# Larger backward loads, a padded copy of wo, and backward stores issued by GpSimd, in a transformer block's forward and backward kernel

**Chip, cores, metric.** One core of one Trainium2 chip. Times are device microseconds (us) of that core for one execution; a median is quoted with the lowest and the highest run. TensorE is the matmul engine (PE in the profile, PEld its weight loads), VectorE is DVE, ScalarE is ACT, GpSimd is POOL, SyncE is SP (SPq: its queue of DMA issues). The granted clock is the share of TensorE's full clock that the chip allowed.

## The reference

A block of layer norm, 16-head attention (head size 28) and a gated MLP, side by side, on 2048 rows of 448 values. The kernel returns the output and the gradients of the input and of all five weight tensors, in bf16.

```python
S, D, H, F = 2048, 448, 16, 1792
xn = layernorm(x)
y  = x + attention(xn, wqkv) @ wo + (silu(xn @ w_gate) * (xn @ w_up)) @ w_down
out, vjp = jax.vjp(f, x, wqkv, wo, w_gate, w_up, w_down)
grads = vjp(grad_out)
```

## The kernel before

A forward pass spills what the backward pass needs to device memory. Then come 512 backward steps, 128 for each of four groups of heads: ScalarE forms two exponentials, VectorE multiplies them by the backward scores into a tile `ds_sb`, and a DMA transposition, or TensorE for every fourth step, makes `dsT` of it. Between the steps other work is filled in: first the output y, then weight gradients and the gradient of the input. SyncE issues all DMAs that matter here, the transpositions among them. Loads are registered with a due step and dripped into its queue; stores are held for two steps.

```python
def drop():                      # once per step
    ...
    while slow and credit > 0:
        _, _, o, i = slow.pop(0)
        SP.dma_start(out=o, in_=i)
        credit -= size(o)

def load_q(g, qc):
    t = new_q(g, qc)
    drip(("q", g, qc), [(t[:, i:i + 2], QD_d[g, qc, :, i:i + 2]) for i in (0, 2)], 128 * g + 4 * qc - 4)

def store(o, i):
    held.append((now + 2, o, i))
    flush(0 if now < NB else 10 ** 9)

def flush(upto):
    while held and held[0][0] <= upto:
        _, o, i = held.pop(0)
        SP.dma_start(out=o, in_=i)

def dst_dma(b, ds, qi):          # three steps of four
    if qi == 0:
        dsT[b] = bk.tile([P, 4, 2, 4, P], BF16, name="dsT", bufs=3)
    SP.dma_start_transpose(out=dsT[b][:, qi].rearrange("p j kt s -> p (j kt) s"),
                           in_=ds[:].rearrange("p j k -> p (j k)"))

# in ew(k), the elementwise part of a step
ds = dss[k - 1] = kq.tile([P, 2, 512], BF16, name="ds_sb", bufs=10)
for j in range(2):
    DVE.tensor_tensor(out=ds[:, j], in0=dps.pop((k - 1, j))[:], in1=est[k - 1][:, j], op=ALU.mult)

# in y_unit, 16 times
y = yp.tile([P, D], BF16, name="y")          # a pool of two buffers
DVE.tensor_tensor(out=y[:], in0=ps[:, :D], in1=yts[ti][:], op=ALU.add)
store(out0_d[:, 4 * ch + ti, :], y[:])
```

The softmax here doesn't subtract the row's maximum and nothing guards it: scores larger than these inputs give would overflow.

## Time and profile before

| | before |
|---|---|
| time, median of three runs | 1447.26 us (1446.37 to 1447.65) |
| profiled span, granted TensorE clock | 1448.2 us, 0.985 |
| busy share PE, DVE, ACT, POOL | 92%, 80%, 87%, 25% |

VectorE's 80% is an average that hides its 92.5% in the later backward steps: each stretch must be read by itself.

### The profile page before, as it was taken

Reading aid. Unit: us, or ns where it says so; the run is one execution under the profiler, and the core shown is the slowest. Engines: PE = TensorE matmul, PEld = TensorE weight load, DVE = VectorE, ACT = ScalarE, POOL = GpSimd, SP = SyncE. Lnnn points to the kernel's source line nnn. Section 1 sums busy time; section 2 is a strip of 40 time slices with the busy share of each in tenths; the row PEclk is TensorE's granted clock in tenths of the full one; section 3 lists DMA queues with packets and bytes.
Section 4 is the critical chain, followed back from the end, with each engine's and each line's share of the span. In section 5 each row is a group of like instructions: output and inputs, shape, how many; then the busy total and the mean of one; then the engine's idle time right before and its main releaser. Section 6 shows DMA issues by size and latency. Waiting matters only on the chain. (4 is left out here: it accounts for less than half of the span.)

```text
span 1448.2 us, 34787 instructions
## 1 busy us (share of the span) xinstructions
PE 1335.4 (92%) x12708; PEld 539.9 (37%) x12708; DVE 1151.7 (80%) x1997; ACT 1261.2 (87%) x2193; POOL 363.1 (25%) x486
## 2 busy tenths in 40 slices
PE   5899999999999999889899989999999999999996
PEld 2333333333333333333333433433343344443343
DVE  6677756666667666488898988888889999989988
ACT  5788988988999999778898988899989999989974
POOL 6475514453344453110101101101001011010005
PEclk9999999999999999989999999999999999999998
DMA  6797947796778676799999999999999999999971
GB/s 153 161 211 184 220 112 166 177 203 154 157 170 184 143 175 145 193 211 204 217 218 211 208 225 181 211 211 212 232 193 192 208 215 230 199 197 201 204 145 60
DMA packets 701763, 271.18 MB, mean 187 GB/s; under 512 B 620224, under 2 KB 676248, under 8 KB 701592
## 3 DMA queue, kind: packets, MB, share of 16 engines
q1 hardware_dynamic: 696616, 262.83, 88.5%
q0 software_dynamic: 3568, 5.83, 1.8%
q8 instruction: 100, 1.64, 0.5%
q14 instruction: 71, 0.58, 0.1%
q10 hardware_dynamic: 1408, 0.30, 0.1%
HBM read 65.04 MB, written 59.90 MB: 86 GB/s over the span
## 5 line engine op out<-in xcount | busy, mean ns | idle before, releaser
L840 DVE TENSOR_TENSOR ds_sb<-db,e_sb 128x512 bf16<-128x512 f32 x1024 | 646.8, 684 | 54.7 <-issue 25.5
L834 ACT ACTIVATE e_sb<-sb 128x512 bf16<-128x512 f32 x1024 | 555.0, 612 | 66.1 <-PE db L818 49.8
L611 ACT ACTIVATE eT<-s_w 128x1024 bf16<-128x1024 f32 x256 | 263.5, 1029 | 47.0 <-PE s_ps L608 44.0
L613 ACT ACTIVATE eT<-s_ps 128x512 bf16<-128x512 f32 x512 | 280.5, 613 | 0.0
L818 PE MATMUL db<-kd,qd 32*128 32x512 bf16 x1024 | 236.1, 385 | 7.2 <-DVE ds_sb L840 6.4
L810 PE MATMUL sb<-kd,qd 32*128 32x512 bf16 x1024 | 210.7, 388 | 7.4 <-DMA qd<-QD_d 3.5
L959 POOL TENSOR_TENSOR dq_acc<-dq_acc,dq_st 128x256 f32<-128x256 f32 x64 | 46.4, 726 | 571.6 <-ACT dq_st L957 571.6
L917 PE MATMUL acc<-ds_sb,qd 128*32 128x512 bf16 x1024 | 161.1, 391 | 0.0
L913 PE MATMUL acc<-e_sb,qd 128*32 128x512 bf16 x1024 | 159.0, 391 | 1.3 <-DVE dw_o L527 1.3
L900 ACT COPY dsT<-db 128x1024 bf16<-128x1024 bf16 x128 | 130.2, 1017 | 14.1 <-PE db L895 13.5
L379 POOL TENSOR_TENSOR nn<-nn,ag 128x512 f32<-128x512 f32 x56 | 71.2, 1271 | 249.6 <-DVE ag L377 240.9
L608 PE MATMUL s_ps<-QQ,KK 32*128 32x512 bf16 x512 | 125.3, 385 | 3.9
L1127 PE MATMUL genb<-wguT,dau_c 128*128 128x448 bf16 x448 | 117.5, 355 | 6.3 <-ACT dq_st L957 3.9
L608 PE MATMUL s_w<-QQ,KK 32*128 32x512 bf16 x512 | 100.3, 387 | 11.8 <-ACT eT L611 10.2
L810 PEld LDWEIGHTS <-qd 32*128 32x128 bf16 x1024 | 48.2, 91 | 152.4 <-issue 140.6
L420 PE MATMUL gen<-xn_t,f_sp 128*128 128x448 bf16 x416 | 91.8, 354 | 2.6 <-DVE nn L394 1.7
L944 PE MATMUL genb<-dsT,kd 128*32 128x256 bf16 x2048 | 79.1, 274 | 6.0 <-DVE y L1079 4.2
L420 PEld LDWEIGHTS <-f_sp 128*128 128x128 bf16 x640 | 55.7, 98 | 75.9 <-issue 32.0
L895 PE MATMUL db<-ident_bf,ds_sb 128*128 128x128 bf16 x1032 | 79.0, 220 | 1.1 <-DVE ds_sb L840 1.1
L895 PEld LDWEIGHTS <-ds_sb 128*128 128x128 bf16 x1032 | 67.9, 98 | 24.6 <-issue 6.0
L380 POOL TENSOR_TENSOR nn<-nn,tt 128x512 f32<-128x512 f32 x56 | 72.0, 1286 | 4.4
L450 PE MATMUL gen<-eT,VS 128*32 128x512 bf16 x1024 | 68.4, 384 | 4.3 <-DVE nn L394 2.2
(163 smaller groups left out, 1879.5 us busy)
## 6 DMA issues: line engine op xcount, KB each, us to landing
F_d<-hda SPq DMA_DIRECT2D x56, 384.0 KB
dau_c<-F_d SPq DMA_DIRECT2D x56, 256.0 KB
h_c<-F_d SPq DMA_DIRECT2D x24, 256.0 KB
qd<-QD_d SPq DMA_DIRECT2D x24, 256.0 KB
dsT<-ds_sb SPq DMA_TRANSPOSE x383
dc<-dqkvT_d SPq DMA_DIRECT2D x12, 384.0 KB
wT_d<-wT_f SPq DMA_DIRECT2D x14, 256.0 KB
KD_d<-qk_sp SPq DMA_DIRECT2D x7, 512.0 KB
```

The source lines that it names most:

```text
L420: PE.matmul(ps[:, :D], lhsT=fsp[fc][:, t // 4, w, t % 4, :], rhs=rhs[:, t, :], start=(t == 0), stop=(t == NT - 1))
L608: PE.matmul(sp4[hh], lhsT=KK[g][r:r + HP, kt * P:(kt + 1) * P], rhs=QQ[g][r:r + HP, qsl], start=True, stop=True, tile_position=(r, 0))
L611: ACTE.activation(out=e2[0][:], in_=wide[:], func=ACT.Exp, scale=SCALE)
L613: ACTE.activation(out=e2[1][:, j], in_=sp4[2 + j], func=ACT.Exp, scale=SCALE)
L810: PE.matmul(s_ps[:], lhsT=qside[g, qc][r:r + HP, 0, qi * P:(qi + 1) * P], rhs=kside[g, kc][r:r + HP, 0, :], start=True, stop=True, tile_po ...
L818: PE.matmul(d_ps[:], lhsT=qside[g, qc][r:r + HP, 1, qi * P:(qi + 1) * P], rhs=kside[g, kc][r:r + HP, 1, :], start=True, stop=True, tile_po ...
L834: ACTE.activation(out=est[k][:, j], in_=sps.pop((k, j))[:], func=ACT.Exp, scale=SCALE)
L840: DVE.tensor_tensor(out=ds[:, j], in0=dps.pop((k - 1, j))[:], in1=est[k - 1][:, j], op=ALU.mult)
L895: PE.transpose(ps[:, c, :], ds[:, c // 4, (c % 4) * P:(c % 4 + 1) * P], ident_bf[:])
L900: ACTE.copy(out=o, in_=ps[:])
L913: PE.matmul(a[r:r + HP, :], lhsT=sp4[:, 1, r:r + HP], rhs=e[:, j, :], start=first, stop=last, tile_position=(0, r), skip_group_check=True)
L917: PE.matmul(a[r:r + HP, :], lhsT=sp4[:, 0, r:r + HP], rhs=ds[:, j, :], start=first, stop=last, tile_position=(0, r), skip_group_check=True)
```

## The change

Its intent is to take issues off SyncE: loads in one to three pieces in place of two to five, and all stores that go through `flush` issued by GpSimd. `wo`, which was loaded in four pieces into a zeroed tile, is written once in padded form to device memory in the forward pass and loaded in one piece.

```diff
+    wo_d = dram.tile([P, G, D], BF16)
...
             woT_load(3)
+            SP.dma_start(out=wo_d[:], in_=wo_pad[:, :, :D])
...
-        drip(("q", g, qc), [(t[:, i:i + 2], QD_d[g, qc, :, i:i + 2]) for i in (0, 2)], 128 * g + 4 * qc - 4)
+        drip(("q", g, qc), [(t[:], QD_d[g, qc])], 128 * g + 4 * qc - 4)
...
-        drip(("k", g, kc), [(t[:, 0:2], KD_d[g, kc, :, 0:2]), (t[:, 2], KD_d[g, kc, :, 2])], 128 * g + 16 * kc - 4)
+        drip(("k", g, kc), [(t[:], KD_d[g, kc])], 128 * g + 16 * kc - 4)
...
             _, o, i = held.pop(0)
-            SP.dma_start(out=o, in_=i)
+            POOL.dma_start(out=o, in_=i)
...
-                               for a, b in ((0, 2), (2, 4), (4, 6), (6, 7))], due)
+                               for a, b in ((0, 4), (4, 7))], due)
...   (x, o, fT, w_down, the gate and up weights and dau likewise in bigger pieces)
-    POOL.memset(wo_sb[:], 0.0)
-    drip(("y", 0, 1), [(wo_sb[HP * pv(hh):HP * pv(hh) + DH, :, :], wo_v[hh]) for hh in range(4)], 50)
+    drip(("y", 0, 1), [(wo_sb[:], wo_d[:])], 50)
```

More of the change, by code (lines that the diff above doesn't have):

```diff
@@ L871 @@
     w2 = bk.tile([P, 4, 2, P], BF16, name="dqT", bufs=1)
-    drip(("f",), [(fT[:, sc], fT_d[:, sc]) for sc in range(4)], 10)
+    drip(("f",), [(fT[:, a:a + 2], fT_d[:, a:a + 2]) for a in (0, 2)], 10)
     def late_dw(c):
@@ L1038, in load_y @@
             x_c = yp.tile([P, 4, D], BF16, name="x_c")
-            drip(("y", ch, half), [(x_c[:, a:a + 2], x_d[:, 4 * ch + a:4 * ch + a + 2, :]) for a in (0, 2)], due)
+            drip(("y", ch, half), [(x_c[:], x_d[:, 4 * ch:4 * ch + 4, :])], due)
             ych[ch, 2] = x_c
@@ L1042, in load_y @@
             o_c = yp.tile([P, G, 512], BF16, name="o_c")
-            drip(("y", ch, half), [(o_c[:, a:a + 2], OT_d[ch, :, a:a + 2]) for a in (0, 2)], due)
+            drip(("y", ch, half), [(o_c[:], OT_d[ch])], due)
             ych[ch, 3] = o_c
@@ L1047 @@
     wo_sb = yp.tile([P, G, D], BF16, name="wo_sb", bufs=1)
-    POOL.memset(wo_sb[:], 0.0)
     wd_v = B_w_down.rearrange("(fc p) d -> p fc d", p=P)
-    drip(("y", 0, 0), [(wd_sb[:, a:a + 2, :], wd_v[:, a:a + 2, :]) for a in (0, 2, 4, 6)], 35)
+    drip(("y", 0, 0), [(wd_sb[:, a:a + 4, :], wd_v[:, a:a + 4, :]) for a in (0, 4)], 35)
     load_y(0, 0)
     load_k(0, 2)
-    drip(("y", 0, 1), [(wd_sb[:, a:a + 2, :], wd_v[:, a:a + 2, :]) for a in (8, 10, 12)], 50)
-    drip(("y", 0, 1), [(wo_sb[HP * pv(hh):HP * pv(hh) + DH, :, :], wo_v[hh]) for hh in range(4)], 50)
+    drip(("y", 0, 1), [(wd_sb[:, a:a + 3, :], wd_v[:, a:a + 3, :]) for a in (8, 11)], 50)
+    drip(("y", 0, 1), [(wo_sb[:], wo_d[:])], 50)
     load_y(0, 1)
@@ L1104, in load_w @@
         w = dxs["w", fq] = dxs["pool"].tile([P, 5, 2, D], BF16, name="wguT")
-        drip(("dx", 0, fq), [(w[:, i - f0], wT_d[:, i, :, :D]) for i in range(f0, f1)], due)
+        drip(("dx", 0, fq), [(w[:, i - f0:min(i + 2, f1) - f0], wT_d[:, i:min(i + 2, f1), :, :D]) for i in range(f0, f1, 2)], due)
     def load_dx(ch, fq):
@@ L1111, in load_dx @@
         d = dxs["pool"].tile([P, 5, 2, 512], BF16, name="dau_c")
-        drip(("dx", ch, fq), [(d[:, i - f0], F_d[ch, :, i, 1:3, :]) for i in range(f0, f1)], now + 16)
+        drip(("dx", ch, fq), [(d[:, i - f0:min(i + 2, f1) - f0], F_d[ch, :, i:min(i + 2, f1), 1:3, :]) for i in range(f0, f1, 2)], now + 16)
         dxs[ch, fq] = d
```

## The prediction

> **What bounds the kernel now.** I read the page first (shares, forty slices), then cut the span into stretches, then the waits, then the queue of the engine that the change relieves. The backward pass is 512 steps, each with two exponentials on ScalarE and two multiplications by the backward scores on VectorE (tile ds_sb), and it fills about 620 to 1400 us. The first fence has, per stretch, the busy time of PE, PEld, DVE, ACT and POOL, the granted clock and the DMA share.
>
> ```profile
> 650.00:900.00 250.00, 229.56 (x2586) 94.02 (x2583) 220.07 (x358) 220.11 (x408) 21.77 (x30) 0.97 1.08 209
> 1000.00:1300.00 300.00, 288.34 (x3341) 122.55 (x3341) 277.53 (x472) 275.64 (x516) 26.85 (x37) 1.00 1.09 208
> ```
>
> Three engines are near full in both: no single one is the bound. But the early stretch, where the forward output y is computed between the steps, is looser: TensorE is 91.8% busy against 96.1%, VectorE 88.0% against 92.5%, ScalarE 88.0% against 91.9%. Counting ds_sb multiplications, the early stretch has 322 in 250 us, so 1.55 us a step; 1000 to 1300 us has 398 in 300 us, 1.51 us a step; 1100 to 1200 us has 139 in 100 us, 1.44. GpSimd is nearly idle (21.8 of 250 us). So something costs the early stretch some per cent, and a granted clock of 0.97 is only part of it.
>
> The waits of that stretch that a DMA ended (us in total, times, longest) are few:
>
> ```profile
> DVE y L1079 <- DMA out_dram<-y: 5.7, 3, 2.3
> DVE ds_sb L840 <- DMA dsT<-ds_sb: 5.0, 6, 1.7
> PEld L810 <- DMA kd<-KD_d: 2.5, 1, 2.5
> PEld L1071 <- DMA o_c<-OT_d: 1.3, 1, 1.3
> PEld L944 <- DMA dsT<-ds_sb: 1.2, 2, 0.9
> ```
>
> From 900 to 1400 us the same list names a single wait on a DMA, of 0.4 us. Why are they late here? SyncE's queue, in order of time (start, us, what):
>
> ```profile
> 837.86 1.23 SPq L827 DMA_TRANSPOSE dsT<-ds_sb  x1
> 839.14 0.58 SPq L767 DMA_DIRECT2D kd<-KD_d  x1
> 839.81 1.23 SPq L827 DMA_TRANSPOSE dsT<-ds_sb  x1
> 841.10 0.58 SPq L767 DMA_DIRECT2D kd<-KD_d  x1
> 841.78 1.45 SPq L827 DMA_TRANSPOSE dsT<-ds_sb  x1
> 843.28 0.57 SPq L767 DMA_DIRECT2D h_c<-F_d  x1
> 843.95 1.23 SPq L827 DMA_TRANSPOSE dsT<-ds_sb  x1
> 845.23 0.58 SPq L800 DMA_DIRECT2D out_dram<-y  x1
> 845.90 1.24 SPq L827 DMA_TRANSPOSE dsT<-ds_sb  x1
> ```
>
> One issue follows the other with some 0.05 us between: the queue is never empty. A transposition takes SyncE 1.23 us at least, a plain copy 0.57. Summed over 650 to 900 us: 121 transpositions 168 us, 108 copies 64 us, semaphore instructions 3 us, and about 0.05 us around each of them; that is the whole 250 us. The tile y shows the lag (duration in ns least, median and greatest, then first and last start in us):
>
> ```profile
> L1079 DVE TENSOR_TENSOR y<-genb,yt x16: 625/625/626, 707.6 to 895.9; 128x448 bf16<-128x448 f32 x16
> L800 SPq DMA_DIRECT2D out_dram<-y x16: 570/574/668, 719.2 to 902.4; - x16
> ```
>
> The first y is finished at 708.2 us and its store is issued at 719.2: 11 us, of which the program's own two-step delay is 3. I also matched every transposition with the multiplication that makes its input. In the five 50 us slices from 650 us on, the issue starts on average 9.2, 7.0, 6.5, 8.3 and 6.1 us after the input is ready; from 1100 to 1200 us it is 0.6 and 1.5. With 2.2 us (median) from the end of the issue to the landing, one in ten lands over 14.5 us after its input in the slice from 650. The ring of ds_sb has ten buffers, so one comes round after ten steps of 1.55 us, 15.5 us. The backlog therefore just reaches the ring, and that is the 5.0 us line. The waits that are put down to "DVE ds_sb" on SyncE's own list (81.6 us in this stretch) I don't believe: that input had been ready for 6 to 9 us.
>
> **What the Trainium skill says.** "DMA: Bandwidth & Descriptors", section "Issuing engines are not separate DMA queues": all DMAs run on the same 16 engines whoever issues them, and another issuer saves only sequencer time, which is usually small beside the DMA. The trace agrees that the sequencer's time is all there is to save (an issue of 0.57 us against 1.7 us more to the landing of a y store), but here that time is not small: the sequencer is full. The same page, "SWDGE vs HWDGE vs iDMA": GpSimd's descriptors are written by software on its cores, so those stores occupy GpSimd. In the trace GpSimd spends 0.53 to 0.84 us on each of its forward loads, which land 3.1 to 4.2 us after issue. "SBUF — State Buffer", section "SBUF: two separate sides": such a DMA can starve while VectorE holds the shared port pair in a two-port mode. The 1024 multiplications read one operand from PSUM, and nothing in the trace before shows such a stall; I count it as a risk.
>
> **The change, part by part.** I compared the two instruction orders. TensorE, VectorE and ScalarE run the same instructions in the same order; only their waits differ.
>
> - Stores to GpSimd: 24 dkv, 12 dqT, 16 y, 16 dwq_o and 8 last weight gradients, 76 issues. Off SyncE: 76 x 0.57 = 43 us. Onto GpSimd: 76 x 0.53 to 0.84 = 40 to 64 us, spread over 800 us in which GpSimd is 9% busy. Its additions into dq_acc (726 ns each, one per four steps) may now stand behind a store for a microsecond; ScalarE needs the buffer dq_st again only some 6 us later, so this is hidden.
> - Bigger loads: dau 56 to 32, h 32 to 16, k 28 to 14, q 24 to 12, weights 14 to 8 and 7 to 4, x and o 8 to 4 each, fT 4 to 2, and wo 4 to 1: 185 to 97. 88 x 0.57 = 50 us off SyncE. Bytes stay the same and SyncE's issue time hardly depends on size (0.37 to 0.57 us for up to 0.9 MB). Each load is placed within a few steps of where it was, some earlier (the k block before step 112 goes at 91).
> - Padded wo: one memset of 1.6 us on an idle GpSimd goes, one 448 KB store joins the forward pass, where no engine waits for it: 0.
>
> Between the first y load and the opening of the next phase (steps 17 to 180) SyncE's copies fall from 110 to 36, so 74 x 0.62 us, with the gap, = 46 us less work in some 250 us. Its demand falls to about 82%, and the backlog should go from 6 to 9 us to 1 or 2, as at 1100 us. Then the five waits above vanish: 5.7 + 5.0 on VectorE and 2.5 + 1.3 + 1.2 on TensorE, 15.7 us. Some fall while another engine has work queued, and part comes back as a wait on the next engine, so I take 70%: 11 us. As a cross-check: 161 steps at 1.51 instead of 1.55 us save 7 us; at 1.44 they save 18. Later than 900 us SyncE has a backlog of 0.5 to 4 us that holds up nobody: 0 to 2 us, I take 1. The end (1400 us on) is VectorE's chain; its four dwq_o stores move into gaps of 1.05 to 1.55 us between GpSimd's pairs of final additions: 0. Sum: 1447 - 12 = 1435 us.
>
> **Rivals.** (1) The backlog never mattered, transfers are hidden anyway, and the early stretch is slow for its clock (0.97) and its y work. For it: the recorded waits are only 15.7 us, 1% of the time, and each may sit beside other slack. Against it: the stretch lacks 4% on all three engines at once. It would give 1444 to 1448. (2) The step was SyncE's all along, and the whole early stretch falls to 1.44 us a step, with some gain to 1050 us too: 18 + 5 us, so 1424. Against it: VectorE would have to be 95% busy, as it is only in the best slice (47.64 of 50 us from 1150), and the clock is lower here. (3) GpSimd becomes the new queue: a store waits in order for its producer or for an earlier landing, dq_acc comes late, ScalarE stalls on dq_st, or larger loads in one piece hold transpositions back at the DMA engines, which are over 100% busy by the page's account (overlapping packets). It would give 1450 to 1465. Against it: 91% idle time, 6 us of slack, unchanged bytes.
>
> **Range and chances.** From the middle of 1435 down to the second rival, 1424, and up to the first with a little of the third, 1447. A gain of over 2% needs 1418 or less, 29 us, which is more than the early stretch can lose even at the best pace seen: 4%. A loss of over 2% needs rival 3 in full and more: 2%. Within 2%: 94%.
>
> **What would show it.** Right: SyncE shows real gaps from 650 to 900 us; y stores are issued 3 to 5 us after their y and by GpSimd; no wait on dsT, y or kd in that stretch; about 335 multiplications there in place of 322, and nearly the same count as before from 1100 us on. Wrong: SyncE idle and the step count unchanged (rival 1); ScalarE waiting for GpSimd's dq_acc, or landings of transpositions well over 2.2 us after issue (rival 3); a gain spread evenly over all stretches, which would mean that the queue delayed things in a way that my list of waits doesn't show.

## More of the kernel before

The page's list of DMA queues has, per queue, packets, megabytes, and the share of the 16 DMA engines' time. The hardware queue carries what SyncE issues, the software queue what GpSimd issues.

```profile
q1 hardware_dynamic: 696616, 262.83, 88.5%
q0 software_dynamic: 3568, 5.83, 1.8%
```

So SyncE's queue carries nearly all the traffic.

## The result and the profile after

The changed kernel is correct and took 1441.29 us (median of 4 runs, 1439.69 to 1441.88), against 1447.45 us (1446.37 to 1451.47, 4 runs) for the kernel before in the same rounds: a ratio of 0.9951, 95% interval 0.9930 to 0.9971. Ratios here are the mean time of one kernel's runs over that of the other's of the same rounds, so not quite the ratio of the medians. The forecast was 1435.0 with a range from 1424 to 1447: the gain was 6 to 7 us in place of 12. Both profiled runs are fast ones with the same mean clock, 0.985 (spans 1448.2 and 1440.1 us).

The two stretches of the prediction, in the kernel after (busy us of PE, PEld, DVE, ACT, POOL, then clock, DMA share, GB/s):

```profile
650.00:900.00 250.00, 234.83 (x2684) 97.87 (x2680) 227.32 (x374) 227.37 (x421) 41.48 (x66) 0.99 1.15 217
1000.00:1300.00 300.00, 288.42 (x3332) 122.26 (x3328) 278.27 (x474) 274.88 (x513) 40.69 (x60) 0.99 1.08 206
```

The early stretch rose from 229.6 to 234.8 us on TensorE and from 220.1 to 227.3 on VectorE; the later one stands where it was. Counted as in the prediction, by 50 us slices, the early stretch has 332 `ds_sb` multiplications where it had 322. The waits that a DMA ended, from 620 to 900 us (us in total, times, longest), are down to this:

```profile
DVE ds_sb L842 <- DMA dsT<-ds_sb: 3.4, 4, 1.0
PE genb L946 <- DMA dsT<-ds_sb: 0.2, 1, 0.2
```

The waits on y, kd and o_c are gone, 9.5 us by the prediction's list. The tile y (duration ns least, median, greatest; first and last start us):

```profile
L1080 DVE TENSOR_TENSOR y<-genb,yt x16: 624/624/626, 702.7 to 886.3; 128x448 bf16<-128x448 f32 x16
L802 POOL DMA_DIRECT2D out_dram<-y x16: 557/557/579, 705.2 to 889.3; - x16
DMA to landing us min/median/max: 2.8/4.4/6.0
```

The first y is done at 703.3 us and GpSimd issues its store 1.9 us later, where SyncE took 11 us. But SyncE's own queue did not become loose (start us, us, what; neighbouring issues of one kind are joined):

```profile
702.01 0.58 SPq L769 DMA_DIRECT2D h_c<-F_d  x1
702.69 6.83 SPq L829 DMA_TRANSPOSE dsT<-ds_sb  x4
709.57 0.58 SPq L769 DMA_DIRECT2D h_c<-F_d  x1
710.25 4.71 SPq L829 DMA_TRANSPOSE dsT<-ds_sb  x3
715.01 0.58 SPq L769 DMA_DIRECT2D x_c<-in_A_x_dram  x1
715.70 5.36 SPq L829 DMA_TRANSPOSE dsT<-ds_sb  x3
```

There are still no gaps, although only one copy comes to about three transpositions. Four transpositions take 6.83 us, 1.7 us each, three take 5.36. The tile view of the transpositions from about 650 to 900 us says the same (least, median and greatest ns), first before, then after:

```profile
L827 SPq DMA_TRANSPOSE dsT<-ds_sb x121: 1231/1240/2838, 650.3 to 899.7; - x121
```

```profile
L829 SPq DMA_TRANSPOSE dsT<-ds_sb x126: 1231/1377/3667, 647.8 to 899.1; - x126
```

The least is the same, the median is longer by 0.14 us and the greatest by 0.8. The page's queues after:

```profile
q1 hardware_dynamic: 672576, 255.35, 87.1%
q0 software_dynamic: 7024, 13.82, 4.1%
```

**Where the time came from.** I laid the 512 steps of the two traces side by side, by the end of each step's second multiplication, and followed the lead of the kernel after. Up to step 32 it is 0.6 us and constant. It then grows where the kernel before stood waiting: by 6.5 us between steps 32 and 64 (the ring of `ds_sb`, then y), 1.9 at 96 to 104 (y), 2.1 at 136 to 144 (kd) and 1.5 at 168 to 176 (y), 12.0 in all, and to 9.6 at step 176. In between the steps mostly take the same time in both. But it also shrinks: by 1.6 us between steps 64 and 96, 0.8 between 104 and 136, 0.5 between 144 and 168, 2.9 in all. These losses come at 742 to 749, 798 and 844 to 857 us of the trace after. Three of VectorE's four remaining waits on `dsT` lie just before them (0.8 us at 741, 0.9 at 797, 0.6 at 836); the fourth (1.0 at 773) has no loss beside it. Another 1.6 us are lost by step 300, where the clock after dips to 0.93 (900 to 925 and 1000 to 1025 us). From there to the end the lead stands at 8.0 us: 0.6 + 12.0 - 2.9 - 1.6, rounded.

A rival for part of the 12.0 us is the clock. From 650 to 900 us it stood at one half for 13.6 us before (6.8 from 673 us, 3.4 from 779, 3.4 from 844) and for 3.4 us after, means of 0.97 and 0.99. The later dips after, of 3.4 us each, go with losses of some 1 us each. By that measure up to 3 of the 12.0 us may be the clock's, an estimate; no run separates them. That the change gains at all rests on the ratios over many runs, not on this pair of traces.

### The profile page after: what moved, and what is told of

It reads as the page before. It is cut to its first block, busy times and chain, and to the rows that moved or that the text cites. A ratio compares the mean times of both kernels' runs of the same rounds, so it can differ in the third digit from the quotient of the medians.

```text
span 1440.1 us, 34682 instructions
## 1 busy us (share of the span) xinstructions
PE 1326.3 (92%) x12647; PEld 541.0 (38%) x12708; DVE 1151.8 (80%) x1997; ACT 1261.5 (88%) x2193; POOL 403.6 (28%) x561
## 3 DMA queue, kind: packets, MB, share of 16 engines
q1 hardware_dynamic: 672576, 255.35, 87.1%
q0 software_dynamic: 7024, 13.82, 4.1%
```

## The experiments

Twelve kernels ran, in three batches, each on one chip with runs of the kernel before. All gave correct results, the added stores going to a scratch tensor. The chips differ by a few us, so only ratios within a batch are compared.

| kernel | ratio to before | 95% interval | median us (before in the same batch) |
|---|---|---|---|
| stores to GpSimd alone | 0.9965 | 0.9942 to 0.9987 | 1445.21 (1451.47) |
| bigger loads and padded wo alone | 0.9992 | 0.9976 to 1.0009 | 1449.33 (1451.47) |
| before, four y buffers | 1.0005 | 0.9983 to 1.0027 | 1450.85 (1451.47) |
| after, 74 tiny stores on SyncE, early | 1.0005 | 0.9988 to 1.0023 | 1452.47 (1451.47) |
| after, 74 tiny stores on SyncE, late | 1.0014 | 0.9990 to 1.0038 | 1454.43 (1450.31) |
| after, 11 ds_sb buffers | 0.9929 | 0.9907 to 0.9951 | 1442.60 (1450.31) |
| after, loads on GpSimd too | 1.0283 | 1.0250 to 1.0316 | 1496.48 (1450.31) |
| stores alone, small loads on GpSimd too | 1.0360 | 1.0315 to 1.0405 | 1509.76 (1450.31) |
| after, 74 tiny stores on GpSimd, early | 1.0155 | 1.0121 to 1.0190 | 1477.15 (1453.95) |
| before, 11 ds_sb buffers | 0.9996 | 0.9968 to 1.0024 | 1450.96 (1453.95) |
| after, again | 0.9946 | 0.9923 to 0.9969 | 1445.25 (1453.95) |
| after, 11 ds_sb buffers, again | 0.9935 | 0.9910 to 0.9961 | 1445.85 (1453.95) |

### Each half alone

The kernel before with only the stores moved:

```diff
 def flush(upto):
-            SP.dma_start(out=o, in_=i)
+            POOL.dma_start(out=o, in_=i)
```

> The kernel before with one part of the change: the backward stores go to GpSimd, all loads stay in small pieces on SyncE. My theory (the gain is made of single waits that vanish): the three waits of VectorE on the stores of y (5.7 us before) vanish, 5 us; the one of 2.5 us on kd and most of those on dsT (5.0 us) may shrink, because 37 of 110 copies leave SyncE's queue in that phase. Time 1440 to 1443, that is 4 to 7 us less than before, and no wait on y in the list. Transpositions from 650 to 900 us take SyncE 1.39 us on average as before, if it is the big loads that stretched them to 1.66 in the changed kernel. Rival (the loads made the gain): within 2 us of before. Rival (stores from the other queue compete with the transpositions): their mean goes to 1.6 us or more here.

The kernel after with that line put back, so bigger loads and padded wo alone:

> The other part alone: bigger loads and one padded wo load, stores stay on SyncE. My theory: kd and dsT waits go (about 3 to 5 us gained), y stores still go out behind some transpositions, so a part of the 5.7 us on y stays; time 1441 to 1445. Transpositions on SyncE from 650 to 900 us are stretched to 1.6 us or more if the big loads ahead of them in the same queue are the reason. Rival (the stores made the gain): within 2 us of before, and y waits of 4 us or more. If the stores on the other queue stretch the transpositions, their mean stays below 1.45 us here.

Measured: 0.9965 and 0.9992. The stores give 3.5 of the change's 5 thousandths, and their interval lies below 1; the loads give an unresolved 0.8. With the stores moved, no wait on y is left, and the ring hardly waits, less than in the kernel after (3.4 us), while kd and o_c (1.0 us) still do:

```profile
PEld L810 <- DMA kd<-KD_d: 1.2, 1, 1.2
DVE ds_sb L840 <- DMA dsT<-ds_sb: 0.3, 1, 0.3
```

With the loads alone y and the ring still wait:

```profile
DVE y L1080 <- DMA out_dram<-y: 6.1, 2, 4.0
DVE ds_sb L842 <- DMA dsT<-ds_sb: 4.5, 3, 2.3
```

So the gain is mainly the stores' way out, by the point values and the waits; the two intervals overlap slightly. The lag of the transpositions behind their inputs says nothing of this by itself: in the five slices of 50 us from 650 us it averages 8.1, 5.8, 5.4, 3.8 and 2.7 us with the loads alone and 6.9, 6.8, 6.5, 7.4 and 3.4 with the stores alone, so on the whole it is shorter where no gain is resolved. The transpositions take 1.44 us on average with the stores alone and 1.52 with the loads alone, against 1.39 before and 1.66 after, so it is the two parts together that stretch them most.

### Is a longer ring as good as a shorter queue?

The kernel before, with two more buffers for y, so that VectorE need not wait for the store:

```diff
-            y = yp.tile([P, D], BF16, name="y")
+            y = yp.tile([P, D], BF16, name="y", bufs=4)
```

> The kernel before with four buffers for y in place of two, nothing else: this takes away the wait for the late y store without moving any DMA. My theory: the gaps of 2.1, 1.6 and 1.5 us that the changed kernel closes at steps 64, 100 and 172 close here too, so 4 to 6 us less than before: 1441.5 to 1443.5. Rival (the y waits sit beside other waits, and the gain came from the relieved queue as a whole): less than 2 us, and the same multiplications are late for another reason.

Measured: 1.0005; the expected gain did not come. The waits on y vanished, but the list of waits from 620 to 900 us (us, times, longest) shows where they went:

```profile
DVE ds_sb L840 <- DMA dsT<-ds_sb: 9.0, 9, 2.0
PEld L944 <- DMA dsT<-ds_sb: 2.0, 2, 1.1
PEld L810 <- DMA kd<-KD_d: 1.5, 1, 1.5
```

The ring of `ds_sb` waits 9.0 us where it had waited 5.0. A step that isn't held at y runs on and is held at the next thing behind the same queue. The opposite test, later, was one more `ds_sb` buffer in the kernel before (and two `dx` buffers fewer at the very end, for room):

```diff
-            ds = dss[k - 1] = kq.tile([P, 2, 512], BF16, name="ds_sb", bufs=10)
+            ds = dss[k - 1] = kq.tile([P, 2, 512], BF16, name="ds_sb", bufs=11)
...
-        dx = tw.tile([P, D], BF16, name="dx", bufs=4)
+        dx = tw.tile([P, D], BF16, name="dx", bufs=2)
```

> The kernel before with eleven ds_sb buffers in place of ten (and two dx buffers in place of four at the very end to make room). Theory A (the backlog costs time only where it reaches the ring or the y buffers): the ds_sb waits of 5.0 us fall to under 1.5, the waits of y, kd and o_c stay, ratio 0.995 to 0.999. Rival B (the wait only moves to the next thing behind the queue, as with four y buffers): the y and PE waits grow by what the ds_sb waits lose and the ratio stays at 0.999 to 1.002.

Measured: 0.9996, in the rival's range, though the interval covers both. The waits speak for the rival too:

```profile
DVE y L1079 <- DMA out_dram<-y: 7.9, 3, 3.4
PEld L810 <- DMA qd<-QD_d: 4.2, 1, 4.2
DVE ds_sb L840 <- DMA dsT<-ds_sb: 1.0, 1, 1.0
```

The wait of the ring fell from 5.0 to 1.0 us, and y rose from 5.7 to 7.9 with a new 4.2 us on qd. (The profiled run is that kernel's slowest, 1461.07 us, at a clock of 0.976, so the sums are indicative.) Buffers that are added where one wait is seen move it; moving the stores out of the queue removes it.

### Is it SyncE's issue time?

The kernel after with 74 extra stores of 32 bytes, issued by SyncE between steps 17 and 180, which gives its queue back the number of issues that the change took away there:

```diff
+    tiny_d = dram.tile([80, 64], BF16)
...   (after drop(), in each step k)
+            if 17 <= k < 180 and 74 * (k - 16) // 163 > 74 * (k - 17) // 163:
+                n = 74 * (k - 17) // 163
+                SP.dma_start(out=tiny_d[n:n + 1, 0:16], in_=ident_bf[0:1, 0:16])
```

> The changed kernel with 74 copies of 32 bytes added on SyncE's queue, spread over steps 17 to 180: as many issues as the change took away there, without their bytes. If SyncE's time to issue is the scarce thing (my prediction), the backlog grows by several us over that phase, transpositions land past the ring of ten buffers, waits of VectorE on dsT return, and 4 to 8 us are lost: 1445 to 1449. If SyncE is full only because its transpositions are held back by what is ahead of them at the DMA engines, their stretch shrinks (1.66 towards 1.4 us) to make room, and the time stays within 2 us of the changed kernel, 1440 to 1443.

Measured: 1.0005; the whole gain is lost. The transpositions did shrink, from 1.66 to 1.50 us on average, as the second theory said, but the time did not stay. From 620 to 900 us the ring waits three times as long as in the kernel after, for stores that move no data to speak of:

```profile
L1252 SPq DMA_DIRECT2D tiny_d<-ident_bf x74: 232/422/879, 652.7 to 905.1; - x74
```

```profile
DVE ds_sb L843 <- DMA dsT<-ds_sb: 10.9, 14, 2.0
```

The control puts the same 74 stores at steps 340 to 503, where I believed that SyncE had room:

> The control for e4_tiny: the same 74 copies of 32 bytes on SyncE's queue, but from step 340 to 503, where the changed kernel's backlog is 0.3 to 2.7 us and the ring is far. If an issue costs only where the queue is full and its backlog reaches the ring of ten buffers, nothing is lost: within 2 us of the changed kernel (0.995 of before). If 74 more issues or transfers cost by themselves, 4 us or more are lost, as in e4_tiny (1.0005 of before).

Measured: 1.0014. The control failed: late issues cost as much as early ones. The profiled run (1444.54 us, 10 us under the median, so not typical) lost 6.7 us of its lead between steps 368 and 496. There SyncE's lag behind its inputs grew to 3.9 to 7.7 us on average in the five slices of 50 us from 1150 us, where the kernel after has 0.3 to 3.2 in its trace of the third batch. But from 1100 to 1400 us only 1.8 us of VectorE's waits and 3.7 us of TensorE's (weight loads and matmuls each counted) end with a DMA, and the clock was 0.97 in two slices. How the loss divides between issues and clock stays open. So "SyncE has room later" was wrong at that load, and the early run alone does not show that the early stretch is special.

### Does GpSimd's queue relieve the transpositions?

If a load in SyncE's queue only holds up the transposition behind it, the loads on GpSimd should set it free. The kernel after, and the one with the stores alone, with the loads in `drop` and `have` moved as well:

```diff
-        SP.dma_start(out=o, in_=i)
+        POOL.dma_start(out=o, in_=i)
```

> The changed kernel with its backward loads issued by GpSimd too: SyncE is left with the transpositions. If the transpositions are stretched to 1.66 us because a big load stands ahead of them in the same queue, they take 1.25 to 1.4 us here from 650 to 880 us, SyncE gets real gaps, the backlog falls under 2 us, the last 3.4 us of waits on dsT go, and the time is 2 to 6 us below the changed kernel (0.991 to 0.994 of before). If the DMA engines themselves are full, a transposition keeps 1.6 us and more or lands later, and the time stays within 2 us of the changed kernel. Risk: additions into dq_acc behind a load that waits for a free buffer; then ScalarE waits for GpSimd and it is slower.

> The kernel before, its loads still in small pieces, with loads and stores both issued by GpSimd. SyncE has the transpositions alone, as in e6. If SyncE's queue is what counts, this equals e6 within 2 us, in spite of 88 more issues, which go to an idle engine (88 x 0.55 = 48 us of GpSimd's time). If the size of a load counts by itself (fewer, longer bursts at the DMA engines), it is 2 us or more apart from e6, and the transpositions differ in length.

Measured: 1.0283 and 1.0360, both clearly slower. Both profiled runs are slow (over 1.5% above the kernel's fastest run: 1531.4 us at a clock of 0.952, and 1516.5 at 0.958), so from them I take only what is far beyond that. With no load left in SyncE's queue its transpositions in the early stretch take 2.2 to 2.3 us on average, more than in any other kernel; the first of these kernels:

```profile
L829 SPq DMA_TRANSPOSE dsT<-ds_sb x110: 1231/1426/8343, 648.8 to 900.0; - x110
```

One issue alone held SyncE for 8.3 us, and some transpositions landed up to 30 us after their input. My expectation for the first of them missed: a different issuer does not shield transpositions from loads. The second is not within 2 us of the first but some 11 us slower, with intervals that just touch; the lengths of the transpositions hardly differ.

The last question was whether a transfer costs by being issued or by existing. The 74 tiny stores again, issued by GpSimd at the same steps:

```diff
-                SP.dma_start(out=tiny_d[n:n + 1, 0:16], in_=ident_bf[0:1, 0:16])
+                POOL.dma_start(out=tiny_d[n:n + 1, 0:16], in_=ident_bf[0:1, 0:16])
```

> The kernel after with the same 74 stores of 32 bytes at steps 17 to 180 as in the run that put them on SyncE, but issued by GpSimd. It separates the issue on SyncE from the transfer itself. Theory A (the cost is SyncE's own issue time): ratio as the kernel after, 0.993 to 0.997, and the transpositions of 650 to 880 us last about 1.66 us as after. Rival B (any transfer more, wherever issued, disturbs the transpositions, as the loads moved to GpSimd did): ratio 0.998 to 1.003, and transpositions longer than 1.75 us on average. The bytes are nothing, so if B holds it is the count and not the size.

Measured: 1.0155, worse than either theory's range, on the rival's side. In the early stretch the transpositions (2.02 us on average) and the waits (us, times, longest) grew:

```profile
L830 SPq DMA_TRANSPOSE dsT<-ds_sb x106: 1231/1340/6142, 649.0 to 898.8; - x106
```

```profile
DVE ds_sb L843 <- DMA dsT<-ds_sb: 21.9, 15, 4.0
PE genb L947 <- DMA dsT<-ds_sb: 5.6, 4, 3.4
PEld L947 <- DMA dsT<-ds_sb: 5.5, 4, 3.9
```

and SyncE's queue now reads

```profile
781.06 0.58 SPq L770 DMA_DIRECT2D kd<-KD_d  x1
781.73 5.01 SPq L830 DMA_TRANSPOSE dsT<-ds_sb  x2
786.80 0.58 SPq L770 DMA_DIRECT2D h_c<-F_d  x1
```

Two transpositions take 5.01 us after a load of kd. So a transfer costs though SyncE does not issue it, and the loss with the same stores on SyncE is not shown to be its issue time either. One caution: the clock in this stretch was 0.90 (0.99 after), and in all six runs it was lower over the whole (0.966 to 0.974, against 0.977 to 0.984 of the kernel after on the same chip). So the loss, 28 us over the kernel before in this run, is not all laid to the queue; what lowered the clock is not shown.

### What lengthens a transposition

This came out of the traces after the runs. I joined each of SyncE's issues from 650 to 880 us with the semaphore update of its landing, and sorted transpositions by what was issued before them. The long ones after the change are the second behind a load: load, transposition, transposition.

| kernel | number | mean length of the second transposition, us | load lands after its own issue, median us | end of the transposition's issue minus landing of the load, 10th, 50th, 90th percentile, us |
|---|---|---|---|---|
| before | 26 | 1.43 | 2.95 | -0.39, 0.03, 0.34 |
| stores alone | 34 | 1.56 | 2.77 | -0.26, 0.03, 0.30 |
| bigger loads alone | 28 | 1.94 | 3.56 | -0.26, -0.16, -0.08 |
| after | 35 | 2.19 | 3.75 | -0.25, -0.16, -0.06 |
| after, tiny stores on GpSimd | 33 | 3.19 | 4.77 | -0.27, -0.15, -0.06 |

A second trace of the kernel after, on another chip, gives 35, 2.19 and 3.85 us, and -0.29, -0.16 and -0.07. In the last two rows the issue ends 0.06 to 0.27 us before the load lands in eight of ten cases, whether the load takes 3.75 or 4.77 us: SyncE behaves as if it could not finish issuing the second transposition before the load two places ahead has all but landed. Over the 35 cases after, length and load time correlate at 0.94. When the tiny stores made loads land 1.02 us later, the second transposition became 1.00 us longer. That is an intervention, though not one designed for it. A rival is that busy DMA engines delay both. Against it, the first transposition behind the same loads takes only 1.30 us on average after; but no run excludes it. Nor does the earlier DMA seem to have to stand in SyncE's queue: in the first kernel with all loads on GpSimd, 14 of the 20 transpositions over 3 us end 0.1 to 0.5 us before some DMA of GpSimd's lands, where the 63 landings in these 230 us would give 2 by chance, and none of the 26 under 1.3 us does. That is one slow run, so a hint. What in the chip makes the coupling, I can't show.

It explains most of SyncE's account for 650 to 900 us, number and us:

| kernel | transpositions | copies | both, us |
|---|---|---|---|
| before | 121, 168.0 | 108, 63.6 | 231.6 |
| stores alone | 125, 179.7 | 77, 52.2 | 231.9 |
| bigger loads alone | 123, 186.7 | 73, 44.9 | 231.6 |
| after | 125, 207.6 | 38, 25.2 | 232.8 |
| after, tiny stores on SyncE | 119, 178.0 | 107, 54.3 | 232.3 |
| after, tiny stores on GpSimd | 105, 212.5 | 36, 25.4 | 237.9 |

The copies went down by 38.4 us and the transpositions up by 39.6. The 35 second ones are together 35 x (2.19 - 1.24) = 33 us longer than the median length before, 1.24 us; the 26 second ones before are so by 26 x (1.43 - 1.24) = 5 us. That is 28 us of the 39.6; four more transpositions are another 5.

Why should 32 bytes delay the loads? The page's queues of the two runs give a hint, first with the tiny stores on SyncE, then on GpSimd:

```profile
q1 hardware_dynamic: 672724, 255.35, 86.9%
```

```profile
q0 software_dynamic: 9392, 13.83, 4.0%
```

Against 672576 and 7024 in the kernel after, 74 stores are 148 packets on SyncE's queue, 2 each, and 2368 on GpSimd's, 32 each. The Trainium skill, "DMA: Bandwidth & Descriptors", section "Why a DMA increments its semaphore by 16 and not by 1", says that in a DMA issued by GpSimd all 16 engines report completion, whatever its shape, while a small one from SyncE can run on a single engine. 32 against 2 packets fits that. The same page, "Queues, rings and completion order", has each DMA engine alternate between the queues it has work for. That the packets on all engines delay the loads is then plausible, but no run isolates it.

### The best version

> The changed kernel with eleven buffers in the ring of ds_sb instead of ten (and two for the last output tile instead of four, for room; that may cost up to 1 us at the very end). If SyncE's queue still sets the pace in the changed kernel, one more buffer is a loan of one step and gains 1.5 us at most. If the remaining waits on dsT (3.4 us) are single bursts that one buffer absorbs, 2.5 to 3.5 us are gained against the changed kernel: ratio to before 0.992 to 0.993.

The kernel after with eleven `ds_sb` buffers came out at 0.9929, against 0.9951 for the change alone in an earlier measurement. To settle it, both ran on one chip:

> The kernel after, unchanged, five rounds on this chip: the yardstick for the other three of this batch. Expected ratio 0.993 to 0.997, as in its first timing (0.9951).

> The kernel after with eleven ds_sb buffers, again, now beside the kernel after on the same chip. Theory A (what is left of the backlog after the change still reaches the ring of ten, for 3.4 us): 2 to 4 us faster than the kernel after, ratio to before 0.991 to 0.994. Rival B (its lead in the earlier batch was the chip or the clock): ratio within 0.001 of that of the kernel after.

Measured: 0.9946 and 0.9935, with medians of 1445.25 and 1445.85 us and intervals that overlap for the most part. The second sight doesn't confirm the 2 to 4 us. The change itself is confirmed on a second chip; a version better than it was not found.

## Why the prediction was right or wrong

- **Time and range.** 1441.29 us lies within the range and within 2%. The mechanism named, a SyncE backlog that holds up y and the ring, was right for the waits; the size was about twice what came. That the time fell in the range although the queue did not empty is in part luck.
- **What waits would vanish.** Right for y, kd and o_c. The ring's wait fell from 5.0 to 3.4 us only.
- **The term that was mis-sized.** "I take 70%: 11 us" plus 1 us later. At the places of those waits the steps gained 12.0 us (part of it perhaps the clock's), but 2.9 us came back in the same stretch, in which the queue stayed full and new waits on `dsT` arose. The net is 9.1 us, 58% of 15.7 and not 70%. Later 1.6 us were lost at the clock dips, where I had added 1. That leaves 7.5 us in place of 12. That the new waits cause the 2.9 us is read from their times, not tested.
- **The step that failed.** "Its demand falls to about 82%, and the backlog should go from 6 to 9 us to 1 or 2". SyncE showed hardly any gaps (four over 0.3 us, 3.3 us in all, from 650 to 900 us): its transpositions grew from 168.0 to 207.6 us as its copies fell from 63.6 to 25.2. In the five slices of 50 us from 650 us the start of a transposition lagged its input by 6.3, 6.7, 7.4, 6.9 and 2.7 us on average, against 9.2, 7.0, 6.5, 8.3 and 6.1 before: only the ends of the stretch improved. The premise under it was "SyncE's issue time hardly depends on size (0.37 to 0.57 us for up to 0.9 MB)". That is true of the load's own issue as a rule (0.58 us in the lines shown, though single ones from 650 to 900 us after took up to 1.44) and false of the queue: the second transposition behind a load took 2.19 us in place of 1.43, and ended as the bigger load landed. The y stores were rescued by leaving the queue, not by its emptying. I had taken an engine that is always busy for one whose work is a sum of fixed pieces.
- **Multiplications.** 332 counted against "about 335", up from 322: this came out well although the backlog stayed, since the waits that went were ones at which the lead grew, and perhaps in part by the clock.
- **GpSimd.** Right: its stores cost 0.55 to 0.70 us each on average, its busy time rose from 363 to 404 us, and no wait of ScalarE on it is on record in the backward pass after. The y store came 1.9 to 2.4 us after its y (once 0.3), earlier than the 3 to 5 forecast. The prediction's "0.53 to 0.84 us" for forward loads are means by line; single ones took up to 1.01.
- **Rivals.** The first (the backlog never mattered) is refuted by the change, 0.9930 to 0.9971, and by the stores alone, 0.9942 to 0.9987, though its time, 1444 to 1448, was nearer to the result than the second's 1424. The second asked for 1.44 us a step in the early stretch; 332 multiplications are 1.51. That SyncE sets part of the pace is not excluded, since it stayed full. The third was partly right: transpositions land later (median 2.69 us after the end of the issue over the backward pass, from 2.24, and 2.97 from 2.23 in the early stretch), but the change gains all the same. With more traffic on GpSimd's queue its loss came, 1.6 to 3.6% over before, by late transpositions and not by ScalarE waiting for `dq_acc`.

What stays open: why the early stretch, with hardly a DMA wait left, is still looser than the later one (TensorE 93.9% against 96.1%), what the late tiny stores cost by themselves, and how much of each difference in the traces is the clock's.

## What to carry to other kernels

Read a queue's time as a whole before crediting it for issues removed: where issues follow without a gap, an issue's length may go with somebody else's landing, and the time freed may be filled by the next. Here, moving the stores that a ring of buffers waits for out of a full queue gave a resolved gain (0.9965); making the loads bigger (0.9992) and adding buffers (1.0005, 0.9996), which only moved the wait, did not. A second issuer is not free room: try the traffic in small amounts, since here 76 needed stores on GpSimd gained 5 us, and 74 needless ones beside them lost 30, part of it perhaps by the lower clock.

## What the Trainium skill lacked or had wrong

- "DMA: Bandwidth & Descriptors", section "Issuing engines are not separate DMA queues": another issuer saves only sequencer time, usually small. Here it mattered in both directions: stores on GpSimd gained 0.35% (0.9965), all loads there as well lost 2.8 and 3.6% (1.0283, 1.0360).
- No page gives, for this chip, the time in which SyncE issues a transposition of this size (a comparison with trn3 on the page above has only cycle counts of unnamed earlier generations), or says that its length can go with an earlier DMA's landing: 1.23 us at the least, 2.19 us on average as the second behind a load of 336 to 512 KB, ending 0.06 to 0.25 us before that load lands in eight of ten cases.
- The same page, section "Measured (HBM→SBUF, 128 partitions, SWDGE, issued from GpSimd)", advises batching DMAs to 1 MiB and more. It lacks what bigger loads did to the transpositions in the same queue: going from 128 to 256 KB up to 384 to 512 KB for most loads raised their mean from 1.39 to 1.52 us and gave 0.9992 (0.9976 to 1.0009), no resolved gain. Loads of 1 MiB were not tried.
- The same page, section "Why a DMA increments its semaphore by 16 and not by 1", has all 16 engines report the completion of GpSimd's DMAs whatever their shape, which 32 packets for a store of 32 bytes fit (2 from SyncE), but not the cost: 74 such stores moved the ratio from 0.9946 to 1.0155, where the same on SyncE gave 1.0005 on another chip.
